# Shifting SBUF buffers by pads of 32 to 224 bytes in an attention + two-layer FFN kernel on one core

## The chip, the core and the metric

The kernel runs on one core of a Trainium2 chip. The metric is device time in microseconds (us), the median of three runs. SBUF is addressed here in bytes within a partition (all 128 partitions of a buffer have the same address), and "residue" always means that address modulo 256.

## What is computed

The reference, cut to its core, for 8 batches x 8 heads x 576 tokens, a head size of 64 and so a model width of 512, with an inner width of 1536 in both layers:

```python
kv  = einsum('bhsd,bhse->bhde', k, v)            # linear attention, no softmax
a   = einsum('bhsd,bhde->bhse', q, kv)
a   = a / sqrt(mean(a*a, -1) + 1e-6) * g_norm    # 4608 tokens x 512 after the heads are joined
x   = (sigmoid(a @ w_gate) * (a @ w_val)) @ w_out
g   = x @ w2_gate
out = (g * sigmoid(g) * (x @ w2_val)) @ w2_out
```

## The kernel before

**Arithmetic.** Every matrix product of the two layers is done with each float32 operand split into a rounded "hi" part and a "lo" remainder, and three products (lo*hi, hi*lo, hi*hi). The tokens go in 9 blocks of 512 (`j`). The inner width of one layer is cut into 12 tiles of 128; `PH` makes four stages of them: stage 0 is the first 6 tiles of layer 1 in plain form, stage 1 the other 6 tiles of layer 1, stages 2 and 3 the two halves of layer 2. In stages 1 to 3 two tiles make a pair, and the gate and value products of a pair go through a Winograd-like scheme with seven products (`gv_win`); in stage 3 the out product does too (`out_win`).

**The matmul lines.** A matmul reads two SBUF operands: the stationary one is loaded into the array by a weight load of its own (128 columns of 4 bytes, 512 bytes a partition), and the moving one streams through. The lines are: L645 (`gv_plain`, stage 0; stationary gate/val weights `wgv`, moving `x`, 512 columns), L716 (`gv_win`, stages 1 to 3; stationary `wgv`, moving `x`, 256 columns, 84 matmuls for one pair of one block, called a visit here), L813 (`part_plain`, the out product of stage 0; stationary `wo`, moving `h`, 512 columns), L827 (`part_win`, the out product of stages 1 and 2, 24 matmuls a visit, 512 columns; in stage 1 `wo` is stationary and `h` moves, in stage 2 `h` is stationary and `wo` moves), and L848 (`out_win`, stage 3, 256 columns; `h` stationary, `wo` moving). While one matmul streams, the weight load of the next one reads SBUF beside it.

**Order.** PE's order is written out by hand: each visit's gate/val matmuls come first, then the out matmuls of the visit before (`tail`). From block 4 of stage 0 on, the orders of ScalarE, VectorE and GpSimd are by hand as well. SP's queue issues nearly all DMAs, paced by `tick`.

**Where the buffers lie.** Pools stack up from the left end of SBUF (`hp_` with `h`, then `wk`, `sm`, then `w0p` and `x0p`, which `late_l` replaces after stage 0) and down from the right end (`at`, which `late_r` replaces once the attention is done). A tile begins where the one before it ends; `h` begins at byte 1152, behind constants and DMA scratch, and `late_r` ends at byte 229344. In stage 0, weights, `x` and `wo` lie in `w0p` and `x0p`. In stages 1 to 3 there are six weight slots `s`: slots 0 and 1 lie in `late_r` (called wR below), slots 2 to 5 in `late_l` (wL). A visit of the first pair uses wR, a visit of the other two pairs wL. The 14 parts of `x` lie in `late_r` (xR: tiles x0, x1, x2) for one block and in the `arena` tile of `late_l` (xA) for the next; stage 1 begins with xR, stage 2 with xA, and stage 3 uses xR throughout. So the 81 visits are 18 of xR with wR, 36 of xR with wL, 9 of xA with wR and 18 of xA with wL. The out weights `wo` of slots 0 and 1 are tiles of `late_r`, those of slots 2 to 5 lie in the arena. In stage 3 all out weights lie in the arena; the 42 parts of `h` that a block's three visits make lie in `h` itself (18 parts of one block, 324 matmuls over the stage), in two `raw` slots of `wk` or in the two free `wo` slots of `late_r` by turns (`he`, 336 and 312 matmuls), and in the `xl` slots of `wk` (`hl`, 162 matmuls).

All sizes are multiples of 32 bytes, and within a tile both operands advance by whole multiples of 512 bytes, so the residue of a tile's start is that of each operand taken from it.

Of the kernel before, what the change touches and what calls it, by code (L numbers as in the profile page):

```python
# [9 lines left out]
F32 = mybir.dt.float32  # L10
F32R = mybir.dt.float32r
# [9 lines left out]
def attention_two_ffn(ctx: ExitStack, tc: tile.TileContext, q, k, v, g_norm, weights, out):  # L21
# [10 lines left out]
    DM = H * D  # L32
    DFF = weights[0][0].shape[1] // 2
    NT = B * S
    P = 128
# [3 lines left out]
    KD = DM // P  # L39
    NP = H // 2  # L40
    R = 4
    KB = 1024
# [4 lines left out]
    hp_ = ctx.enter_context(tc.tile_pool(name="hp", bufs=1))  # L47
# [3 lines left out]
    ps_o = ctx.enter_context(tc.tile_pool(name="ps_o", bufs=4, space=PSUM))  # L51
    ps_g = ctx.enter_context(tc.tile_pool(name="ps_g", bufs=4, space=PSUM))

    lo_ctx, at_ctx = ExitStack(), ExitStack()
    w0p = lo_ctx.enter_context(tc.tile_pool(name="w0p", bufs=1))
    x0p = lo_ctx.enter_context(tc.tile_pool(name="x0p", bufs=4))
    at = at_ctx.enter_context(tc.tile_pool(name="at", bufs=1, side="right"))
    late = {}
# [5 lines left out]
    def open_left():  # L64
        lo_ctx.close()
        late["L"] = ctx.enter_context(tc.tile_pool(name="late_l", bufs=1, reuse_waits="tile"))
        for m in range(PH[1][1] + 2, PH[1][1] + 6):
            w_tile(0, m, 0)
        late["arena"] = late["L"].tile([P, 11 * KB], F32R, name="arena")


    ET = mybir.EngineType
# [23 lines left out]
    for j in range(NBLK):  # L96
        t = dr.tile([DM, NB], F32, name=f"xd{j}")
# [148 lines left out]
    def tok_c(tau):  # L246
        if tau >= XT:
            t = xn.pop(tau).rearrange("p h d -> p (h d)")
            z = at.tile([P, DM // SQ, SQ], F32, tag="ta", bufs=TA, name="xz")
            nc.vector.transpose(z.rearrange("p j c -> p (j c)"), t)  # L250
            j, c = divmod(tau, TPB)
            for i in range(P // SQ):
                t0 = c * P + i * SQ
                nc.sync.dma_start(out=xr[j][:, :, t0:t0 + SQ], in_=z[i * SQ:(i + 1) * SQ])
            return
        t = xn.pop(tau).rearrange("p (a b) d -> p a (b d)", b=2)
        ps = bank_for(tau < TPB, "xTp")
        for hp in range(NP):
            nc.tensor.transpose(ps[:, hp, :], t[:, hp, :], ident)  # L259
        x = at.tile([P, NP, P], F32, tag="ta", bufs=TA, name="xT")  # L260
        nc.scalar.activation(x, ps, AF.Identity, scale=gcol)
        j, c = divmod(tau, TPB)
        cs = slice(c * P, (c + 1) * P)
        if j < 2:
            xh, xlo = x_tiles(0, j)
            nc.scalar.activation(xh[:, :, cs], x, AF.Copy)  # L266
            (nc.gpsimd if j == 0 and c < TPB - 1 else nc.vector).tensor_tensor(out=xlo[:, :, cs], in0=x, in1=xh[:, :, cs].bitcast(F32), op=ALU.subtract)
        nc.scalar.dma_start(out=xd[0, j][:, :, cs], in_=x)
# [55 lines left out]
    NRIGHT = 2  # L324
# [16 lines left out]

    wgv, wo, wd = {}, {}, {}

    def w_tile(f, m, c):
        d = wo if c == 2 else wgv
        if (f, m) not in d:
            ph, s = phase_of[f, m]
            pool = w0p if ph == 0 else late["R" if s < NRIGHT else "L"]
            if c == 2 and ph in WOUT:
                a = 3584 * (s // 2)  # L350
                d[f, m] = d[f, m ^ 1] = late["arena"][:, a:a + 3584].rearrange("p (q a) -> p q a", a=2 * P)
            elif c == 2 and ph and s >= NRIGHT:
                a = 7 * KB + (s - NRIGHT) * KB
                d[f, m] = late["arena"][:, a:a + KB].rearrange("p (b a) -> p b a", b=2)
            elif c == 2:
                d[f, m] = pool.tile([P, 2, DM], F32R, tag=f"wo{s}", name=f"wo{f}_{m}")
            elif PH[ph][3]:
                d[f, m] = pool.tile([P, 14, 2, P], F32R, tag=f"wgv{s}", name=f"wgv{f}_{m}")
            else:
                d[f, m] = pool.tile([P, 2, 2, KD, P], F32R, tag=f"wgv{s}", name=f"wgv{f}_{m}")  # L360
        return d[f, m]

    def rounded(f, m, c, buf):
# [36 lines left out]
    def direct(f, m, c):  # L400

        third = (3 * m + c) % 3 == 0

        def buf(t):
            pool = at if third and t != "s" else wk
            if t == "raw":
                return pool.tile([P, DM, 2], U32, tag=t, name=t)
            return pool.tile([P, DM], F32, tag=t, name=t)

        load, ops_, st = rounded(f, m, c, buf)  # L410

        def dst(b):
            t = w_tile(f, m, c)
            return (t[:, b], st["u"]) if c == 2 else (t[:, c, b], st["u"].rearrange("p (k a) -> p k a", k=KD))

        def hi():
            h, u = dst(0)
            nc.scalar.activation(h, u, AF.Copy)

        def lo():  # L420
            h, u = dst(0)
            (nc.vector if m == 0 and c < 2 else nc.gpsimd).tensor_tensor(out=dst(1)[0], in0=u, in1=h.bitcast(F32), op=ALU.subtract)

        return load, ops_ + [hi, lo]
# [113 lines left out]
    def place(f, m):  # L538

        E = 14 * 2 * P  # L540

        def load_gv():
            t = w_tile(f, m, 0).rearrange("p q k a -> p (q k a)").bitcast(F32)
            nc.sync.dma_start(out=t, in_=wd[f, m][:, :E])

        def load_o():
            t = w_tile(f, m, 2).rearrange("p b a -> p (b a)").bitcast(F32)
            nc.sync.dma_start(out=t, in_=wd[f, m][:, E:])

        return load_gv, load_o  # L550
# [3 lines left out]
    xt, xc = {}, {}  # L554
    HB = NB // 2

    def x_load(ph, j, b):
        for i in (b, b + 7):
            t = x_tiles(ph, j)[i // 5][:, i % 5].rearrange("p k a -> p (k a)").bitcast(F32)
            nc.sync.dma_start(out=t, in_=xc[j][:, i * DM:(i + 1) * DM])  # L560

    def x_tiles(ph, j):
        if (ph, j) not in xt:
            if PH[ph][3]:
                s = "RL"[((ph - 1) * NBLK + j) % 2]
                if ph in WOUT and j:
                    xt[ph, j] = x_tiles(ph, 0)
                elif s == "L":
                    xt[ph, j] = [late["arena"][:, i * 5 * DM:min(i * 5 + 5, 14) * DM].rearrange("p (c k a) -> p c k a", k=2, a=HB) for i in range(3)]
                else:  # L570
                    xt[ph, j] = [late[s].tile([P, 5 - i // 2, 2, HB], F32R, tag=f"x{i}", name=f"x{i}") for i in range(3)]
            else:
                xt[ph, j] = [x0p.tile([P, KD, NB], F32R, tag="x", name=f"x{b}") for b in range(2)]
        return xt[ph, j]
# [55 lines left out]
    ht, ops, part, pd = {}, {}, {}, {}  # L630


    h_all = hp_.tile([P, 2, 2, 3, HB], F32R, name="h")
    h_at = [0]

    def gv_plain(ph, j, m, tick):
# [23 lines left out]
    def h_places():  # L660
        if not hw:
            raw = [wk.tile([P, 4, HB], F32R, tag="raw", name="he") for _ in range(2)]
            own = [late["R"].tile([P, 4, HB], F32R, tag=f"wo{i}", name="he") for i in range(2)]
            hw["E"] = raw, own
            flat = h_all.rearrange("p a b c d -> p (a b c) d")
            far = [wk.tile([P, 2, HB], F32R, tag="xl", bufs=3, name="hl") for _ in range(3)]
            hw["L"] = [[flat[:, 6 * p + 2 * i:6 * p + 2 * i + 2] for i in range(3)] for p in range(2)] + [far]
            hw["n"] = 0
        return hw

    def gv_win(ph, j, m, tick, ahead=nop):
# [76 lines left out]
        gated(v[:, 0], v[:, 0], g)  # L748
        if ph in WOUT:
            pl = h_places()  # L750
            p = (m - PH[ph][1]) // 2
            E, Lt = pl["E"][pl["n"] % 2], pl["L"][p]
# [407 lines left out]
    for ph, (f, m0, n, win) in enumerate(PH):  # L1160
# [4 lines left out]
        for at_, (j, ms) in enumerate(visits):  # L1165
# [6 lines left out]
            for i in ms:  # L1172
# [6 lines left out]
                m = m0 + i  # L1179
# [15 lines left out]
                if win:  # L1195
                    ahead = nop
                    if tail and tail[0] in WOUT and tail[2] + 2 == PH[tail[0]][1] + PH[tail[0]][2]:
                        parts = parts_of(tail)
                        ahead = parts.pop(0)
# [22 lines left out]
        if not win:  # L1222
            held = []
            early.__exit__(None, None, None)
            early = tc.manual_schedule(engines={ET.PE, ET.Activation, ET.DVE, ET.Pool, ET.SP})
            early.__enter__()
            finish(parts_of(tail), 0, 0)
            tail = None
            open_left()
            for s in range(NRIGHT, PH[ph + 1][2], 2):  # L1230
                put_place(ph + 1, s, 0, 1 + s // 2)
                if s == NRIGHT:
                    for e in range(2):
                        w_need((f, PH[ph + 1][1] + s + e, 0))
                    for store in held:
                        store()
                    held = None
                put_place(ph + 1, s, 2, 2 + s // 2)
# [31 lines left out]
```

## Time and profile before

| | us |
|---|---|
| median of 3 runs (1805.06 to 1805.45) | 1805.35 |
| span of the profiled execution (first to last instruction) | 1803.8 |
| PE matmul busy, of that span | 1781.5 (99%) |
| PE weight loads busy | 1630.9 (90%) |
| VectorE, ScalarE, GpSimd busy | 1059.3, 659.9, 682.9 |
| L716 visits, stages 1 to 3 (6804 matmuls) | 549.3 + 274.2 |
| L645, stage 0 gate/val (1296 matmuls) | 316.3 |
| L813, L827, L848 out products (648, 1296, 1134 matmuls) | 164.5; 310.8; 148.6 |

A busy PE does not say at what rate matmuls follow each other: matmuls overlap in the pipeline, and the mean duration of one in the table of groups (282 ns for 256 columns) is longer than the distance from one to the next. That distance is read from the chain of waits, which merges an unbroken run of matmuls into one piece and gives its time and count: 9.94 us for 84 matmuls is 118.3 ns for each.

### The profile page before, as it was taken

To read this page: it belongs to the slowest core of one execution; us is meant where nothing else is said; L and a number is where in the kernel's file an instruction comes from. 1 tells how busy PE (TensorE), PEld (TensorE's weight loads), DVE (VectorE), ACT (ScalarE), POOL (GpSimd) and SP (SyncE) were. 2 spreads that over 40 slices of the span, in tenths; PEclk is the share of its full clock that TensorE was granted. 3 is DMA by queue.
4 is the path that set the end of the run, shared out by engine and by line. 5 is a ranking of instruction groups with operands and counts; after the bars stand their busy time and mean duration, and the time that the engine had idled before them with its cause. 6 is when DMAs were issued, how large, how long until landed. Compare 5 with 4: busy or idle time off the path is not lost.

```text
span 1803.8 us, 31990 instructions
## 1 busy us (share of the span) xinstructions
PE 1781.5 (99%) x12358; PEld 1630.9 (90%) x12358; DVE 1059.3 (59%) x1754; ACT 659.9 (37%) x1349; POOL 682.9 (38%) x748
## 2 busy tenths in 40 slices
PE   7899999999999999999999999999999999999999
PEld 6788888888889999999999999999999999999998
DVE  6766566654336667666666566655553555555555
ACT  4663233333233333333333443333432333333332
POOL 1644445421013343342433443333441344444444
PEclk9999999999999999999999999999999999999999
DMA  9968785456326542433449755555568634344432
GB/s 291 264 171 230 222 221 161 133 146 229 105 94 257 181 135 94 157 110 115 145 139 402 271 191 178 181 180 185 186 233 304 216 129 129 129 129 129 129 129 71
DMA packets 274825, 320.40 MB, mean 178 GB/s; under 512 B 95856, under 2 KB 193392, under 8 KB 271984
## 3 DMA queue, kind: packets, MB, share of 16 engines
q1 hardware_dynamic: 259504, 305.24, 52.3%
q10 hardware_dynamic: 15168, 13.11, 2.5%
q8 instruction: 97, 1.59, 0.4%
q14 instruction: 56, 0.46, 0.1%
HBM read 191.14 MB, written 127.14 MB: 176 GB/s over the span
## 4 chain that ended last, share of the span: by engine, by line
PE 95%; DMA 2%; DVE 1%; ACT 1%; SPq 0%; POOL 0%; issue 0%; DVEq 0%; ACTq 0%
PE gv L716 45%; PE o L827 17%; PE gv L645 16%; PE o L813 8%; PE o L848 7%; PE ops L212 1%; DMA raw<-in_moe_w_gate_dram 1%; PE kvps L162 1%; DMA raw<-in_moe_w_out_dram 1%; DMA qm<-in_q_dram 0%; PE xTp L259 0%; DMA pl<-pd 0%; SPq L109 0%; DMA xd<-xT 0%; PE qTp L196 0%
## 5 line engine op out<-in xcount | busy, mean ns | idle before, releaser
L716 PE MATMUL gv<-x,wgv 128*128 128x256 f32 x4536 | 549.3, 282 | 0.0
L716 PEld LDWEIGHTS gv<-x,wgv 128*128 128x128 f32 x4536 | 545.5, 189 | 2.8 <-DVE v L332 0.2
L645 PE MATMUL gv<-x,wgv 128*128 128x512 f32 x1296 | 316.3, 395 | 3.7 <-ACT x L266 2.7
L645 PEld LDWEIGHTS gv<-x,wgv 128*128 128x128 f32 x1296 | 241.3, 189 | 55.6 <-ACT x L266 3.2
L716 PEld LDWEIGHTS gv<-arena,wgv 128*128 128x128 f32 x2268 | 273.6, 190 | 2.4
L716 PE MATMUL gv<-arena,wgv 128*128 128x256 f32 x2268 | 274.2, 282 | 0.0
L332 DVE TENSOR_TENSOR u<-u,gv 128x512 f32<-128x512 f32 x162 | 110.9, 684 | 259.9 <-PE gv L716 247.7
L704 POOL TENSOR_TENSOR h<-v,h 128x512 fp32r<-128x512 f32 x54 | 75.0, 1389 | 241.5 <-ACT h L700 241.2
L813 PE MATMUL o<-h,wo 128*128 128x512 f32 x648 | 164.5, 397 | 0.0
L689 ACT ACTIVATE w<-v 128x256 f32<-128x256 f32 x81 | 33.9, 418 | 312.3 <-DVE v L332 305.0
L813 PEld LDWEIGHTS o<-h,wo 128*128 128x128 f32 x648 | 120.0, 188 | 26.7 <-issue 0.3
L704 POOL TENSOR_TENSOR h<-w,h 128x512 fp32r<-128x512 f32 x54 | 70.8, 1311 | 139.5 <-ACT h L700 138.9
L653 DVE TENSOR_TENSOR sg<-sg,gv 128x512 f32<-128x512 f32 x54 | 36.9, 684 | 114.3 <-PE gv L645 114.3
L827 PE MATMUL o<-arena,h 128*128 128x512 f32 x432 | 103.6, 395 | 0.0
L827 PE MATMUL o<-h,arena 128*128 128x512 f32 x432 | 103.3, 394 | 0.0
L827 PEld LDWEIGHTS o<-arena,h 128*128 128x128 f32 x432 | 79.9, 188 | 17.9
L827 PEld LDWEIGHTS o<-h,arena 128*128 128x128 f32 x432 | 80.1, 188 | 17.5
L760 POOL TENSOR_TENSOR he<-w,he 128x256 fp32r<-128x256 f32 x27 | 20.0, 740 | 186.5 <-ACT he L759 186.5
L848 PE MATMUL o<-arena,he 128*128 128x256 f32 x648 | 82.1, 281 | 0.0
L689 ACT ACTIVATE v<-g 128x256 f32<-128x256 f32 x81 | 33.8, 418 | 131.5 <-DVE g L332 131.5
L332 DVE TENSOR_TENSOR g<-u,gv 128x512 f32<-128x512 f32 x81 | 55.6, 687 | 43.5 <-PE gv L716 42.0
L700 ACT ACTIVATE h<-w 128x512 fp32r<-128x512 f32 x54 | 34.1, 631 | 124.9 <-PE o L827 87.0
(145 smaller groups left out, 2643.2 us busy)
## 6 DMA issues: line engine op xcount, KB each, us to landing
wgv<-wd SPq DMA_DIRECT2D x18, 1792.0 KB, 9.9
x<-xc SPq DMA_DIRECT2D x126, 256.0 KB, 4.2
pl<-pd SPq DMA_DIRECT2D x80, 256.0 KB, 4.0
pd<-ye SPq DMA_DIRECT2D x72, 256.0 KB, 2.7
xc<-arena SPq DMA_DIRECT2D x70, 256.0 KB, 3.3
wd<-raw SPq DMA_DIRECT2D x63, 256.0 KB, 2.9
xc<-x SPq DMA_DIRECT2D x56, 256.0 KB, 3.6
raw<-in_moe_w_gate_dram SPq DMA_DIRECT2D x24, 512.0 KB, 4.5
```

The source lines that it names most:

```text
L162: nc.tensor.matmul(kvps[b][e * D:(e + 1) * D, hp, :D], lt, rt, start=(r == hp == 0), stop=(r == R and hp == NP - 1), skip_group_check=True)
L332: nc.vector.tensor_tensor(out=out, in0=a, in1=b, op=ALU.add)
L645: nc.tensor.matmul(ps, w[:, e, a, kk, :], x[b][:, kk, :], start=(n == 0), stop=(n == 3 * KD - 1))
L653: nc.vector.tensor_tensor(out=sg, in0=sg, in1=bank[1], op=ALU.mult)
L689: nc.scalar.activation(o, t[:, 0], AF.Silu if f else AF.Sigmoid)
L700: nc.scalar.activation(t[:, 0], v, AF.Copy)
L704: nc.gpsimd.tensor_tensor(out=t[:, 1], in0=v, in1=t[:, 0].bitcast(F32), op=ALU.subtract)
L716: nc.tensor.matmul(ps[:, e], w[:, l, kk], xs[r // 5][:, r % 5, kk], start=(fresh and e == n == kk == 0), stop=(not more and e == 1 and n = ...
L760: nc.gpsimd.tensor_tensor(out=hs[z][:, 1], in0=x, in1=hs[z][:, 0].bitcast(F32), op=ALU.subtract)
L813: nc.tensor.matmul(ps, l, r, start=(fresh and t == 0), stop=(last and t == 2))
L827: nc.tensor.matmul(ps, l, r, start=(fresh and e == t == 0), stop=(last and e == 1 and t == 2))
L848: nc.tensor.matmul(ps[:, t], h[:, r, cs], w[:, Ax[a] + 7 * l], start=(start and t == n_ == 0), stop=(stop and t == 1 and n_ == 2), skip_gr ...
```

## The change

A helper `shifted` allocates a tile with some elements ahead of it and behind it that nobody uses, and returns the part between. `LINE` is 8 elements, 32 bytes. `h` moves up by 128 bytes and a 224-byte tile follows it, so everything left of the middle moves up by 352 bytes; the first weight tile of stage 0 gets 160 bytes ahead, weight slot 2 gets 128 ahead, the arena 32 ahead, weight slot 1 gets 32 behind, and x2 of `late_r` 224 behind. No instruction, wait or DMA is added or taken away in the kernel's own code.

The residues that follow, each worked out by adding up the tile sizes:

| buffer | before | after |
|---|---|---|
| stage 0: wgv, wo, x | 0, 0, 0 | 0, 0, 0 |
| h | 128 | 0 |
| tiles of wk (raw, xl, u, v, w, s ...) | 128 | 224 |
| wL | 0 | 224 |
| wR | 224 | 224 |
| xA and the out weights in the arena | 0 | 0 |
| xR | 224 | 0 |
| wo slots of late_r (and he in them) | 224 | 0 |

The stationary operand's residue less the moving one's is written as a difference below. The gate/val visits before: xR with wR 0, xR with wL +32, xA with wR -32, xA with wL 0; after: -32 in all four. The out products before: L813 128; L827 128 with arena weights, 96 or -96 with `wo` of `late_r`; after: 0 in all of them. L848 before: 128, and -32 for the 312 matmuls with `he` in `late_r`; after: 0 with `h` itself and with `he` in `late_r`, -32 with `raw` and `hl`.

```diff
+    def shifted(pool, cols, dtype, by, name, tag=None):
+        ahead, after = by if isinstance(by, tuple) else (by, 0)
+        t = pool.tile([P, ahead + cols + after], dtype, name=name, **({"tag": tag} if tag else {}))
+        return t[:, ahead:ahead + cols]
+
+    LINE = 8
+    H_AT, ARENA_AT, X_AFTER = 4 * LINE, LINE, 7 * LINE
+    RIGHT, LEFT = {(1, 0): (0, LINE)}, {2: 4 * LINE}
+    FIRST = {(0, 0): 5 * LINE}
...
-        late["arena"] = late["L"].tile([P, 11 * KB], F32R, name="arena")
+        late["arena"] = shifted(late["L"], 11 * KB, F32R, ARENA_AT, "arena")
...
+    def w_shift(ph, s, c):
+        if ph:
+            return RIGHT.get((s, c // 2), 0) if s < NRIGHT else LEFT.get(s, 0)
+        return FIRST.get((s, c // 2), 0)
...
-                d[f, m] = pool.tile([P, 14, 2, P], F32R, tag=f"wgv{s}", name=f"wgv{f}_{m}")
+                d[f, m] = shifted(pool, 28 * P, F32R, w_shift(ph, s, c), f"wgv{f}_{m}", f"wgv{s}").rearrange("p (q k a) -> p q k a", k=2, a=P)
...
-                    xt[ph, j] = [late[s].tile([P, 5 - i // 2, 2, HB], F32R, tag=f"x{i}", name=f"x{i}") for i in range(3)]
+                    xt[ph, j] = [shifted(late[s], (10 - i // 2 * 2) * HB, F32R, (0, X_AFTER * (i // 2)), f"x{i}", f"x{i}").rearrange("p (c k a) -> p c k a", k=2, a=HB) for i in range(3)]
...
-    h_all = hp_.tile([P, 2, 2, 3, HB], F32R, name="h")
+    h_all = shifted(hp_, 12 * HB, F32R, H_AT, "h").rearrange("p (b e s a) -> p b e s a", b=2, e=2, s=3)
+    hp_.tile([P, 7 * LINE], F32, name="gap")
```

The tiles `wo`, the stage 0 `wgv` and the `he` tiles in the `wo` slots go through `shifted` in the same way.

## Rows read from the trace of the kernel before

**Rows 1.** The page: busy time of the engines, TensorE's granted clock, the chain.
```profile
PE 1781.5 (99%) x12358; PEld 1630.9 (90%) x12358; DVE 1059.3 (59%) x1754; ACT 659.9 (37%) x1349; POOL 682.9 (38%) x748
PEclk9999999999999999999999999999999999999999
PE 95%; DMA 2%; DVE 1%; ACT 1%; SPq 0%; POOL 0%; issue 0%; DVEq 0%; ACTq 0%
```

**Rows 2.** Busy time by stretch: stretch, its length, engines (instructions), clock, DMA.
```profile
138.00:230.00 92.00, 91.21 (x593) 75.72 (x592) 51.84 (x85) 32.27 (x58) 39.20 (x64) 1.00 0.85 225
230.00:548.00 318.00, 318.00 (x1511) 261.93 (x1510) 165.35 (x256) 104.13 (x188) 94.89 (x125) 1.00 0.53 154
554.00:1450.00 896.00, 895.98 (x6290) 837.46 (x6289) 548.85 (x888) 333.08 (x674) 342.46 (x288) 1.00 0.54 191
```

**Rows 3.** The chain from 579 us, stage 1: start, duration, matmuls in a piece.
```profile
579.59 9.94 PE gv L716 x84
589.53 5.57 PE o L827 x24
595.11 9.80 PE gv L716 x84
604.90 5.57 PE o L827 x24
610.48 10.07 PE gv L716 x84
620.55 5.61 PE o L827 x24
626.16 10.06 PE gv L716 x84
...
641.80 10.07 PE gv L716 x84
```

**Rows 4.** The chain from 1134 us, stage 2.
```profile
1150.63 5.60 PE o L827 x24
1156.22 9.90 PE gv L716 x84
1166.12 5.60 PE o L827 x24
1171.72 10.07 PE gv L716 x84
1181.79 5.62 PE o L827 x24
```

**Rows 5.** The chain from 490 us, the end of stage 0.
```profile
490.65 2.79 PE o L813 x12
493.44 5.45 PE gv L645 x24
498.89 2.79 PE o L813 x12
501.69 5.46 PE gv L645 x24
```

**Rows 6.** The chain in stage 3, from 1473 us and from 1518 us.
```profile
1473.42 2.85 PE o L848 x24
1476.27 8.63 PE gv L716 x72
...
1518.29 2.81 PE o L848 x24
```

**Rows 7.** Busy time inside four visits of stage 1, columns as in group 2.
```profile
645.00:651.00 6.00, 6.00 (x53) 6.00 (x52) 3.22 (x6) 0.80 (x2) 1.92 (x3) 1.00 0.00 1
598.00:604.00 6.00, 6.00 (x54) 6.00 (x53) 3.37 (x6) 0.80 (x2) 0.60 (x1) 1.00 0.69 226
629.00:635.00 6.00, 6.00 (x53) 6.00 (x52) 5.38 (x10) 1.00 (x3) 0.53 (x1) 1.00 0.00 0
```

**Rows 8.** PE in order of time around 200 us, and L813's matmuls before 201 us.
```profile
201.63 3.04 PE L645 MATMUL gv<-x,wgv 128*128 128x512 f32 x12 [0.79 <-DVE xn L242]
...
92.00:201.00 109.00, 33.23 (x126) 22.48 (x124) 1.00 0.76 205
```

**Rows 9.** SP's queue and PE in order of time around 550 us, and DMA landings there.
```profile
545.61 0.90 SPq L544 DMA_DIRECT2D wgv<-wd  x2
...
553.80 20.17 PE L716 MATMUL gv<-x,wgv 128*128 128x256 f32 x168
...
wgv<-wd SPq DMA_DIRECT2D x4, 1792.0 KB, 12.2
```

**Rows 10.** DMA landings from 400 to 425 us, the first loads of wR.
```profile
wgv<-wd SPq DMA_DIRECT2D x2, 1792.0 KB, 9.2
```

More of the change, by code (lines that the diff above doesn't have):

```diff
@@ L355, in w_tile @@
             elif c == 2:
-                d[f, m] = pool.tile([P, 2, DM], F32R, tag=f"wo{s}", name=f"wo{f}_{m}")
+                d[f, m] = shifted(pool, 2 * DM, F32R, w_shift(ph, s, c), f"wo{f}_{m}", f"wo{s}").rearrange("p (b a) -> p b a", b=2)
             elif PH[ph][3]:
-                d[f, m] = pool.tile([P, 14, 2, P], F32R, tag=f"wgv{s}", name=f"wgv{f}_{m}")
+                d[f, m] = shifted(pool, 28 * P, F32R, w_shift(ph, s, c), f"wgv{f}_{m}", f"wgv{s}").rearrange("p (q k a) -> p q k a", k=2, a=P)
             else:
-                d[f, m] = pool.tile([P, 2, 2, KD, P], F32R, tag=f"wgv{s}", name=f"wgv{f}_{m}")
+                d[f, m] = shifted(pool, 4 * KD * P, F32R, w_shift(ph, s, c), f"wgv{f}_{m}", f"wgv{s}").rearrange("p (c b k a) -> p c b k a", c=2, b=2, k=KD)
         return d[f, m]
@@ L662, in h_places @@
             raw = [wk.tile([P, 4, HB], F32R, tag="raw", name="he") for _ in range(2)]
-            own = [late["R"].tile([P, 4, HB], F32R, tag=f"wo{i}", name="he") for i in range(2)]
+            own = [shifted(late["R"], 4 * HB, F32R, w_shift(1, i, 2), "he", f"wo{i}").rearrange("p (c a) -> p c a", a=HB) for i in range(2)]
             hw["E"] = raw, own
```

## The prediction

> **What bounds the kernel now.** I read the page first: PE is busy 99% of the span, at the full granted clock in every slice, and 95% of the chain that ends last is PE [rows 1]. Next comes the busy time by stretch, which tells where that is so: from 230 us to 548 and from 554 to 1450, PE has no idle time worth a number, while the next engine, VectorE, is busy about half or three fifths of it [rows 2]. So from 201.6 us on, behind the last wait of stage 0 that shows [rows 8], a nanosecond less between one matmul and the next is a nanosecond off the end, as long as nobody makes PE wait.
>
> The third view is the chain of waits, because it gives unbroken runs of matmuls with their count. Divide a piece's time by its count and the distance between matmuls comes out. The reader is to see that visits of identical work, 84 matmuls of L716 with 256 columns, take three or four different times, and that these go with the buffers read. Stage 1 runs, in order, xR/wL 9.94, xA/wR 9.80, xA/wL 10.07, xA/wL 10.06, xR/wR 10.07 us [rows 3]. Per matmul that is 118.3, 116.7, 119.9 and 119.9 ns. By difference of residues: +32 gives 118.3, -32 gives 116.7, 0 gives 119.9. In stage 2 the two equal ones stay at 10.07 and -32 gives 9.90 (117.9) [rows 4]; in stage 3, 72 matmuls of xR/wR take 8.63, again 119.9 each [rows 6].
>
> Three things speak for the residues as the cause. xR/wR and xA/wL share no buffer, lie some 100 KB apart, and agree to 0.1%. Inside the visits the other engines and the DMA differ widely without a trace in the rate: in the xA/wL visit VectorE works 5.38 of 6 us, in the xR/wR one 3.22, both at 119.9, and the fast visit has the most DMA of the three, a share of 0.69 [rows 7]. And the clock is 1.00 in all of them.
>
> The 512-column lines show the same thing with another sign. L645 (0/0, difference 0) takes 5.45 to 5.46 us for 24, 227.2 ns; L813 right beside it (difference 128) takes 2.79 for 12, 232.5 ns [rows 5]. L827 takes 5.57 to 5.62 for 24, 232.1 to 234.2 [rows 3, 4]. So for 512 columns an equal residue is the best pair that shows, and for 256 columns it is the worst.
>
> The Trainium skill speaks against this: its page "SBUF — State Buffer", section "SBUF: two separate sides", says that only the port pair shared by VectorE and GpSimd causes contention and that PE never waits on anyone, and "TensorE: Matmul & The Clock Gate", section "Step-by-step: what each phase is for", says that loading the next weights takes no SBUF read bandwidth from the running matmul. By that rule a pad costs and gives nothing and the time stays at 1805.4; the 10.07 against 9.80 of equal visits [rows 3] disagrees.
>
> **The change part by part.** It adds no instruction, no DMA and no wait of its own; it only moves residues. Terms are worked out against the profiled span of 1803.8 us; the median lies 1.55 us above it, and I carry that over.
>
> Gate/val visits (L716). All 81 come to -32. Today's -32 visits take 9.80 in stage 1 (5 of them) and 9.90 in stage 2 (4), mean 9.85; I take the mean and keep both ends. The 18 xR/wR visits fall from 10.07 to 9.85, 4.0 us; the 18 xA/wL ones the same, 4.0; the 36 xR/wL ones from 9.94 to 9.85, 3.2; the 9 xA/wR ones stay. Together 11.2 us. If all settle at 9.80, 81 x 0.05 = 4.1 us more; if all at 9.90, 4.1 less.
>
> Out products of stages 1 and 2 (L827), difference 0 in all 1296. Their six rows here average 5.59 us, 233.1 ns [rows 3, 4]; the nearest row for 512 columns at difference 0 is L645, 227.2. That is 5.9 ns x 1296 = 7.6 us. No row shows L827 itself at 0, so the bounds are 0 (it stays as it is) and 8.5 us (from its slowest rows, 234 against 227.2, a little rounded).
>
> Out products of stage 0 (L813), difference 0. 5.3 ns x 648 = 3.4 us, but 126 matmuls plus some fifteen before them lie ahead of the wait at 201.6 us, where PE waits 0.79 us for VectorE [rows 8]: being faster before it only makes that wait longer. 507 x 5.3 = 2.7 us is left, with bounds 0 and 3.4.
>
> Out products of stage 3 (L848). At 128 today 24 matmuls with `he` in `raw` take 2.85 us, at -32 with `he` in `late_r` 2.81 [rows 6]. The two swap roles in part: 336 + 162 matmuls go from 128 to -32, 0.04/24 us each, 0.8 us gained; 312 go from -32 to 0 and 324 from 128 to 0. No row shows L848 at 0; the nearest is L716's 119.9 ns, against 117.1 and 118.75 now, so 0.9 and 0.4 us are lost. Net 0.5 us lost; bounds 1.3 lost and 0.8 gained (if 0 costs nothing).
>
> Pads as such. A late tile now covers other bytes, and so may wait for another old tile (the arena's first bytes reach into stage 0's weight tile 4). That tile is read before tile 5, on which the arena waits anyway, so this costs nothing. The cover is the slack of the first wL loads: issued by 546.5 us, landing in 12.2 us (median) [rows 9], so at 558.7, and read when the first xR/wR visit ends, some 10.1 us after 553.8 us, at 563.9. About 5 us are free, and PE gets there only 0.2 us earlier. If the new destination residue made these loads slow, up to that slack is hidden; wR, already at 224, landed in 9.2 us [rows 10], so nothing points to it.
>
> Other engines read and write the moved `wk`, but with VectorE at three fifths and PE 1.2% faster, nothing on them comes near the end.
>
> Sum: 11.2 + 7.6 + 2.7 - 0.5 = 21.0 us. 1803.8 - 21.0 = 1782.8 us of span, and a time of 1784.3 us.
>
> **The rivals.**
> (a) The period is longer than 256. All three classes of today hold modulo 512 too, since their differences there are 0, +32 and -32. Modulo 512 the new starts are xR 256, wR 224, xA 0, wL 480, `h` 256, `wo` of `late_r` 256. Then xR/wR and xA/wL still come to -32 (8.0 us), xR/wL and xA/wR land at an unseen 224 (taken as today's middle, 9.94: 0 and 9 x 0.09 = 0.8 us lost), and of the out products only the 432 with `wo` of `late_r` become equal (2.5 us); the rest stay, with 0.5 lost in stage 3. That is 9.2 us, 1796.2. For it: no row tells 256 from 512. Against it: nothing in the rows either; only that the pairs agree at any distance.
> (b) Only the gate/val part works, because L645's 227 ns belong to its own pattern of operands and not to the residue: 11.2 - 0.5, 1794.7. Against it: L645 reads the same shapes with the same alternation of hi and lo parts.
> (c) No effect, because the rates come from something that goes along with the buffers (or by the skill's rule): 1805.4. Against it, all of rows 3 to 6.
> (d) Slower: every gate/val weight slot shares residue 224 with the `wk` tiles that VectorE, ScalarE and GpSimd stream through during the visits, and weight loads pay for it. No row shows this pair; today's xR/wR visits share 224 only with each other. It decides when a visit exceeds its present mean of 9.99 by the 9.8 us that the rest gives, so at 10.11 (120.4 ns). If it cost one more step of the kind seen (10.07 - 9.80) on top of the slowest class, 10.34, the visits lose 81 x 0.35 = 28 us and the time is 1824. Against it: the rate does not follow VectorE's work [rows 7].
>
> **How the numbers follow.** The forecast has a chance of 0.78, (a) 0.08, (b) 0.06, (c) 0.05, (d) 0.03. Its own range, from the ends above, is 21.0 + 4.1 + 0.9 + 0.7 + 1.3, so 1777.3, to 21.0 - 4.1 - 2.7 - 0.8, so 1792.0; the end where L827 gains nothing is (b). To hold 8 in 10, I take 1778.5 to 1796.5, which reaches (a) and (b). A measurement of this kernel can tell about 0.2% (3.6 us) from no change. The forecast, (a) and (b) are all faster: 0.91 with a little of each below the bound taken off; same 0.06; slower 0.03.
>
> **What would show it.** In the profile after: all L716 visits between 9.80 and 9.90 us; L827 at 5.45 for 24 and L813 at 2.73 for 12; L645 unchanged at 5.45; L848's pieces mixed, 2.81 to 2.88 for 24; no new idle time of PE at 563.9 us. Visits of xR/wL and xA/wR that differ from xR/wR and xA/wL would show (a); L827 still at 5.59 would show (b). What would make me wrong outright is a matmul rate that depends on more than the residue and the width, or a PE wait that shows only once PE is faster.

## The result, and the profile after

The changed kernel takes 1782.01 us (median of 4 runs, 1781.64 to 1782.27) where the kernel before took 1805.29 beside it (4 runs): a ratio of 0.9869 [0.9857, 0.9881], 23.3 us less. The forecast was 1784.3. The profiled execution has a span of 1779.9 us against 1803.8. All lines below L645 have moved: L660 is the old L645, L731 the old L716, L828 the old L813, L842 the old L827, L863 the old L848, and L338 and L341 are VectorE's helpers.

The page of the changed kernel, busy time of the engines, answers [rows 1]:

```profile
PE 1757.9 (99%) x12358; PEld 1616.1 (91%) x12358; DVE 1060.0 (60%) x1754; ACT 660.7 (37%) x1349; POOL 683.2 (38%) x748
```

The same instructions, PE just as full, the other engines as busy as before: only the matmuls follow each other faster. The chain of waits shows where (start, duration, matmuls in a piece): stage 1, which answers [rows 3], then stage 2 [rows 4], the end of stage 0 [rows 5] and stage 3 [rows 6].

```profile
549.90 19.60 PE gv L731 x168
...
574.97 9.80 PE gv L731 x84
584.77 5.47 PE o L842 x24
590.24 9.80 PE gv L731 x84
600.05 5.47 PE o L842 x24
605.52 9.80 PE gv L731 x84
...
1126.70 9.80 PE gv L731 x84
1136.50 5.47 PE o L842 x24
...
471.01 2.72 PE o L828 x12
473.73 5.44 PE gv L660 x24
...
1440.43 2.87 PE o L863 x24
1443.30 9.80 PE gv L731 x84
1453.10 2.80 PE o L863 x24
1455.90 8.40 PE gv L731 x72
```

Visits that took 9.80, 9.90, 9.94 or 10.07 us before all take 9.80 now, 116.7 ns a matmul, with any pair of buffers and in all three stages. L842 takes 5.47 for 24, 227.9 ns, where L827 took 5.57 to 5.62. Stage 1 begins 3.9 us earlier (549.90 against 553.80 [rows 9]); the other 20 us come behind it. The first piece is unbroken over both of its visits, so the first loads of wL hold nobody up.

If every matmul is counted from its start to the start of the next one and these distances are summed by line over the whole trace, the difference of spans, 23.9 us, comes apart like this:

| line (before / after) | before, us | after, us | gained | forecast |
|---|---|---|---|---|
| L716 / L731, the visits | 809.25 | 795.65 | 13.6 | 11.2 |
| L827 / L842, out of stages 1, 2 | 302.05 | 295.62 | 6.4 | 7.6 |
| L813 / L828, out of stage 0 | 156.25 | 153.25 | 3.0 | 2.7 |
| L645 / L660, gate/val of stage 0 | 303.9 | 302.8 | 1.1 | 0 |
| L848 / L863, out of stage 3 | 134.0 | 134.1 | -0.1 | -0.5 |
| sum | | | 24.0 | 21.0 |

One new entry stands in the view of waits (total us, times, longest), for PE's weight loads:

```profile
PEld gv L731 <- DVE v L341: 1.5, 5, 0.5
```

Five visits of stage 1 now wait for VectorE, 1.5 us in all (0.2 us in one visit before). The 13.6 us are what is left behind this: 81 visits at 9.80 come to 793.8, which would have been 15.1 us below the 808.9 that the pieces of before add up to.

### The profile page after: what moved, and what is told of

Same layout as the page of the kernel before. It is cut to its first block, busy times and chain, and to the rows that moved or that the text cites. A ratio compares the mean times of both kernels' runs of the same rounds, so it can differ in the third digit from the quotient of the medians.

```text
span 1779.9 us, 31991 instructions
## 1 busy us (share of the span) xinstructions
PE 1757.9 (99%) x12358; PEld 1616.1 (91%) x12358; DVE 1060.0 (60%) x1754; ACT 660.7 (37%) x1349; POOL 683.2 (38%) x748
## 4 chain that ended last, share of the span: by engine, by line
PE 92%; DVE 3%; DMA 2%; issue 1%; ACT 1%; SPq 1%; POOL 1%; DVEq 0%; ACTq 0%
PE gv L731 43%; PE o L842 16%; PE gv L660 15%; PE o L828 8%; PE o L863 7%; PE ops L221 1%; PE kvps L171 1%; DMA raw<-in_moe_w_out_dram 0%; DMA qm<-in_q_dram 0%; PE xTp L268 0%; DVE u L341 0%; DVE pl L341 0%; SPq L118 0%; DMA pl<-pd 0%; DVE u L400 0%
## 5 line engine op out<-in xcount | busy, mean ns | idle before, releaser
L731 PE MATMUL gv<-x,wgv 128*128 128x256 f32 x4536 | 539.7, 279 | 0.4 <-DVE v L341 0.3
L731 PEld LDWEIGHTS gv<-x,wgv 128*128 128x128 f32 x4536 | 535.9, 188 | 3.2 <-DVE v L341 0.8
L660 PE MATMUL gv<-x,wgv 128*128 128x512 f32 x1296 | 313.8, 393 | 3.5 <-ACT x L275 2.4
L660 PEld LDWEIGHTS gv<-x,wgv 128*128 128x128 f32 x1296 | 240.3, 188 | 53.5 <-ACT x L275 2.9
L731 PEld LDWEIGHTS gv<-arena,wgv 128*128 128x128 f32 x2268 | 268.8, 188 | 3.0 <-DVE v L341 0.7
L731 PE MATMUL gv<-arena,wgv 128*128 128x256 f32 x2268 | 269.8, 279 | 0.1
L341 DVE TENSOR_TENSOR u<-u,gv 128x512 f32<-128x512 f32 x162 | 110.9, 684 | 244.8 <-PE gv L731 232.8
L828 PE MATMUL o<-h,wo 128*128 128x512 f32 x648 | 161.9, 394 | 0.3 <-DVE h L338 0.3
L828 PEld LDWEIGHTS o<-h,wo 128*128 128x128 f32 x648 | 120.0, 188 | 25.1 <-DVE h L338 0.7
L842 PE MATMUL o<-h,arena 128*128 128x512 f32 x432 | 101.4, 390 | 0.0
L842 PE MATMUL o<-arena,h 128*128 128x512 f32 x432 | 101.4, 390 | 0.0
L842 PEld LDWEIGHTS o<-h,arena 128*128 128x128 f32 x432 | 79.8, 188 | 15.9
L842 PEld LDWEIGHTS o<-arena,h 128*128 128x128 f32 x432 | 79.8, 188 | 15.9
L863 PE MATMUL o<-arena,he 128*128 128x256 f32 x648 | 82.2, 281 | 0.0
L341 DVE TENSOR_TENSOR g<-u,gv 128x512 f32<-128x512 f32 x81 | 55.6, 687 | 41.4 <-PE gv L731 40.1
L863 PEld LDWEIGHTS o<-arena,he 128*128 128x128 f32 x648 | 79.0, 189 | 0.0
```

The costliest lines, as they stand in the source:

```text
L341: nc.vector.tensor_tensor(out=out, in0=a, in1=b, op=ALU.add)
L660: nc.tensor.matmul(ps, w[:, e, a, kk, :], x[b][:, kk, :], start=(n == 0), stop=(n == 3 * KD - 1))
L731: nc.tensor.matmul(ps[:, e], w[:, l, kk], xs[r // 5][:, r % 5, kk], start=(fresh and e == n == kk == 0), stop=(not more and e == 1 and n = ...
L828: nc.tensor.matmul(ps, l, r, start=(fresh and t == 0), stop=(last and t == 2))
L842: nc.tensor.matmul(ps, l, r, start=(fresh and e == t == 0), stop=(last and e == 1 and t == 2))
L863: nc.tensor.matmul(ps[:, t], h[:, r, cs], w[:, Ax[a] + 7 * l], start=(start and t == n_ == 0), stop=(stop and t == 1 and n_ == 2), skip_gr ...
```

## The experiments

Each edit is shown against the changed kernel; numbers in the code are elements of 4 bytes. In these kernels `GAP` is the length of the tile behind `h`, `X_AHEAD` what x0 gets ahead of it, and keys (0, 0), (0, 1) of `RIGHT` are the weights and the `wo` of slot 0. `SLOT` is what the two `wo` slots of `late_r` get ahead. Values of `LEFT`, `FIRST` and `RIGHT` are left out where they only put another buffer back to its residue, or, in the three sweeps, give each weight slot a residue of its own. Differences are residue of the stationary operand less that of the moving one, as before. Where a rate of a whole line or visit is given to a tenth of a ns, it is a mean of distances between starts.

**Half of the change at a time.** First the gate/val part alone: all visits at -32, while `h`, `wk` and the late `wo` keep the residues of before.

```diff
-    H_AT, ARENA_AT, X_AFTER = 4 * LINE, LINE, 7 * LINE
+    H_AT, GAP, ARENA_AT = 0, 0, 8
+    X_AHEAD, X_AFTER = 8, 56
...
-    hp_.tile([P, 7 * LINE], F32, name="gap")
```

> The gate/val half of the change alone: all weight slots 32 bytes below both x buffers (difference -32), while h, wk and the out weights keep the residues of before (differences 128 and +-96 in the out products). Residue theory: L716 takes 9.80 us a visit, 13.6 us less over 81 visits than before, and L827 stays at 5.57 to 5.62 for 24: 1791.7 us. Sub-question, what sets 9.80 against 9.90 at the same difference: if it is the out product that runs just before the visit, stage 2's visits of wR with the arena's x go back to 9.90 as before, and the time is up to 2.7 us longer, 1794.4; if it is something else, all 81 stay at 9.80. Rival (b) of the prediction gives the whole gain to this half: 1782. Rival that the pads act through something other than the residues: no definite place for the gain, anything from 1782 to 1805.

1791.79 us (1791.13 to 1793.0; before 1806.01), ratio 0.9922 [0.9906, 0.9939]. The chain in stage 1, and two pieces of stage 2:

```profile
578.78 9.80 PE gv L732 x84
588.58 5.58 PE o L843 x24
...
619.34 5.63 PE o L843 x24
624.96 9.90 PE gv L732 x84
...
1149.87 9.80 PE gv L732 x84
1159.67 5.57 PE o L843 x24
```

The visits fall and the out products stay where they were. 9.90 appears again, but not where it did before: all 27 visits of stage 2 take 9.80, and 9.90 stands in 5 visits of stage 1, each behind an L843 at +96 (four more visits behind +96 take 9.80), and in 8 of stage 3. So -32 has two rates, and the stage does not choose between them.

Then the out part alone: gate/val buffers as before, all out products as after.

```diff
+    H_AT, GAP, ARENA_AT = 32, 56, 0
+    X_AHEAD, X_AFTER = 56, 0
```

> The out half alone: h, wk and the out weights as in the changed kernel (difference 0 in L813 and L827), while the gate/val residues are those of before (x and wR at 224, wL and the arena at 0). Residue theory: visits of 10.07, 9.94, 9.80 to 9.90 and 10.07 us as before, L827 at 5.47 for 24 (6.4 us less in all), L813 at 2.72 for 12 (3.0 less), L645 about 1 us less: 1794.8 us, and the gains of both halves add up to the whole, 23.3. Rival (b): 1805.

1796.31 us (1795.81 to 1798.71; before 1806.01), ratio 0.9949 [0.9934, 0.9964]. The chain in stage 1:

```profile
575.29 9.94 PE gv L733 x84
585.23 5.47 PE o L844 x24
590.71 9.80 PE gv L733 x84
600.51 5.46 PE o L844 x24
605.97 10.07 PE gv L733 x84
```

The mirror image: 9.94, 9.80 and 10.07 as before, 5.47 as after. The parts gain 14.2 and 9.7 us, 23.9 together, the whole gain within its error. One thing crosses over: here the nine visits at -32 all take 9.80, those of stage 2 too, where four of them took 9.90 [rows 4]. Of what PE reads, only the operands of the out products between them differ.

**The wk tiles.** `wk` put back to 128, all else as after; this is rival (d), weights that share residue 224 with what the other engines stream through.

```diff
+    H_AT, GAP, ARENA_AT = 32, 32, 8
```

> The changed kernel with the wk tiles at 128 as before in place of 224; all differences of gate/val and of L813 and L827 as in the changed kernel, but he in raw and hl at +128 in L848 as before. Rival (d) of the prediction (weights that share a residue with wk pay for it) would make the visits faster than 9.80; the residue theory leaves them at 9.80 and makes L848 slower by 498 x 1.7 ns = 0.8 us: 1783.

1784.25 us (1783.3 and 1785.19; before 1805.56), ratio 0.9882 [0.9863, 0.9902]. Visits stay at 9.80 (eight of stage 3 at 9.90), and L848's matmuls with `raw` and `hl`, now at 128, go from 116.9 to 118.9 ns. Sharing a residue with `wk` costs nothing; `wk` matters only as an operand of stage 3.

**Other differences.** Three kernels put every buffer at a place of its own, so that one kernel shows many differences: steps of 32 bytes, steps of 16 bytes, and a mixture.

```diff
+    H_AT, GAP, ARENA_AT = 56, 32, 32
+    X_AHEAD, X_AFTER = 48, 32
```

> A sweep of differences in steps of 32 bytes. Gate/val: arena x at 0 with weights at 192, 160, 128 (differences -64, -96, 128), the other x at 96 with the same weights (+96, +64, +32). h at 96: L827 at -96 and +96 with arena weights, +64 and -64 with the others; stage 0's six weight slots at 0 to 160 against x at 0 (L645) and against h at 96 (L813, -96 to +64). Residue theory: +32 comes out at 9.94 a visit as in the kernel before although other buffers and residues make it, 128 at 118.7 ns (9.97), the rest unseen, inside 9.80 to 10.07; L813 at 0 (slot 3) 2.72 for 12, at the others 2.76 to 2.81. Time 1790 to 1806. Rival that absolute residues or the buffers set the rate: no order by difference, +32 anywhere between 9.80 and 10.07.

```diff
+    H_AT, GAP, ARENA_AT = 36, 52, 60
+    X_AHEAD, X_AFTER = 32, 8
```

> The same in steps of 16 bytes. Gate/val: arena x at 0 with weights at 240, 208, 16 (differences -16, -48, +16), the other x at 192 (+48, +16, +80). h at 16: L827 at -16, +16 with arena weights, +48 and -48 with the others; L645 at -16, +16, +48, +80, +112, +144; L813 at -32, 0, +32, +64, +96, +128. Residue theory: +16 takes the same time with both x buffers (two places, two pairs of residues, one difference); if -32 is the bottom of a smooth hollow, -16 and -48 lie between 9.80 and 9.95; if the rate steps in units of 32 bytes, -16 equals 0 or -32. Time 1788 to 1806.

```diff
+    H_AT, GAP, ARENA_AT = 32, 56, 36
+    X_AHEAD, X_AFTER = 8, 48
```

> Differences that are still missing, with h, wk and the order of SP as in the changed kernel: arena x and the arena's out weights at 16, gate/val weights at 0, 96 and 128 (differences -16, +80, +112), the other x at 32 (-32, +64, +96). Residue theory: -32 at 116.7 and +64 at 113.9 to 114.5 in a third and fourth place, +96 at 118.25 as in the first sweep, the new ones unseen; L827 with arena weights at -16 and +16, between 228 and 234. Time 1782 to 1800, since no PE wait comes with it.

1875.33, 1878.92 and 1786.25 us, one run each. The first two missed by 70 us and more, for a reason that has nothing to do with the rates (below, `h` alone). In the second, the differences were not those designed, since the built kernel has every tile's length rounded up to 32 bytes; it adds little. Visits in stage 2 of the first kernel, in order -64, -96, +96 and +64:

```profile
1045.57 9.89 PE gv L733 x84
...
1061.08 10.08 PE gv L733 x84
...
1092.24 9.97 PE gv L733 x84
...
1107.83 9.54 PE gv L733 x84
```

and of the third kernel, a visit at -16 in stage 1, then -16, -32 and +64 in stage 2:

```profile
589.58 9.97 PE gv L733 x84
...
1146.00 9.53 PE gv L733 x84
...
1192.10 10.08 PE gv L733 x84
1207.74 9.54 PE gv L733 x84
```

With other buffers at other residues, +32 gives 118.3 ns again, so the difference counts and not the buffers. But it does not give one rate. Over all kernels here but the second sweep, one matmul of a visit takes:

| difference | rates seen, ns |
|---|---|
| 0 | 120.0 |
| +32 | 118.3 |
| -32 | 116.7, 117.8, 120.0 |
| +64 | 113.3, 117.8 (117.3 where a visit changes its rate, see below) |
| -64 | 117.8 |
| +96; -96 | 117.3, 118.6, 120.0; 120.0 |
| 128 | 118.6 (in the second sweep also 120.0) |
| -16; +80; +112 | 113.3, 118.6; 119.3; 118.7 |

Most visits keep one of these almost from start to end. For 512 columns 0 is the best seen, 227 to 228 ns (up to 230.2 where other differences stand beside it); -64 takes 229.5 to 232, -16 and +16 231.6, the others 232 to 234.

**The fastest rate, +64.** 113.3 ns would save 81 x 0.27, 22 us. So all gate/val buffers went to +64, the rest as after.

```diff
+    H_AT, GAP, ARENA_AT = 32, 56, 48
+    RIGHT = {(0, 0): 24, (0, 1): 48}
```

> The changed kernel with the gate/val weights 64 bytes above x (difference +64) in place of 32 below, all else as in the changed kernel. In the 32-byte sweep the pair at +64 took 114.5 ns for a matmul, in the 16-byte one another pair of buffers at +64 took 113.85. Residue theory: visits of 9.56 to 9.62 us against 9.80, 81 x 0.2 = 16 us less than the changed kernel, 1766 us, if VectorE keeps up; the changed kernel already has five waits of stage 1 for VectorE, 1.3 us in all, and these should grow: up to 8 us if each of the 12 visits to the arena's x in stage 1 lost half of its gain and more, 1774. Rival that 114 ns came from the slower surroundings of those two runs (PE waiting elsewhere, other engines less busy): visits stay at 9.80, 1782.

1782.08 us (1781.62 to 1783.89; before 1805.24), ratio 0.9876 [0.9859, 0.9892]: no better than the change, and the expectation fell. The chain in stage 1, and a visit in stage 3:

```profile
575.11 9.89 PE gv L733 x84
585.01 5.46 PE o L844 x24
590.47 9.89 PE gv L733 x84
...
1478.48 9.53 PE gv L733 x84
```

All 54 visits of stages 1 and 2 took the slow rate, 117.8 (four of them up to a pause, see below); in stage 3 the 17 behind an L848 at -32 took 113.3 and the 8 behind one at 0 took 117.8. That suggested that the out product in between picks the rate. Two kernels tried it: stage 3's out products at +64 too, and the out products of stages 1 and 2 at +96 and -96, behind which the first sweep had shown 113.3.

```diff
+    H_AT, GAP, ARENA_AT = 32, 16, 48
...
+            own = [shifted(late["R"], 4 * HB, F32R, (SLOT[i] + 16, 48), "he", f"wo{i}").rearrange("p (c a) -> p c a", a=HB) for i in range(2)]
...
+            flat = h_t[:, H_AT + 16:H_AT + 16 + 12 * HB].rearrange("p (n d) -> p n d", d=HB)
```

> As the one with +64, and stage 3's out product too: h, the wk slots and the he places stand 64 bytes above the out weights in stage 3 alone (a second view of h, 64 bytes further on), all 1134 matmuls of L848 at +64. Residue theory: L848 falls from 118.4 ns (mean of the changed kernel) to about 114, 1134 x 4.3 = 4.9 us less than with the gate/val part alone, some 1761. Rival that +64 is good for gate/val streams only: no difference from it.

```diff
+    H_AT, GAP, ARENA_AT = 32, 32, 48
+    RIGHT = {(0, 0): 0, (0, 1): 48}
+    SLOT = (48, 0)
+    X_AHEAD, X_AFTER = 0, 16
```

> Gate/val weights 64 bytes above x as in the kernel with +64, but the out products of stages 1 and 2 at -96 and +96 (x and all late out weights at 160, the gate/val weights at 224, h at 0), and in stage 3 the he and hl places 32 below the out weights. In the runs so far +64 has two rates, 113.3 and 117.8 ns, and keeps the one it begins with: 113.3 in 13 of 13 visits behind an L827 at +-96 and in 25 of 29 behind an L848 at -32 or -48, 117.8 in almost all behind a difference of 0. Theory that the out product just before picks the rate: visits of 9.52 us all through, 81 x 0.28 = 23 us less than the changed kernel, L827 at 5.60 in place of 5.47, 54 x 0.13 = 7 us more, L848 some 1 us less, waits for VectorE in stage 1 up to 5 us more: 1765 to 1771 us. Rival that the absolute residues pick it: 117.8 as in the kernel with +64, 1789.

1787.86 us (1786.67 to 1789.02), ratio 0.9905 [0.989, 0.992], and 1784.75 (1783.86 to 1785.5; before 1805.56), ratio 0.9884 [0.9867, 0.99]. Both expectations fell, and so did their rivals. With everything at +64, gate/val and out products of stage 3 run at 117.8 throughout. With out products at +96 and -96, the visits of stages 1 and 2 still take 9.89, though the same differences gave 9.54 in the sweep; behind L848 at -32 again 25 of 25 take 113.3. From stage 1 of the second kernel, and from its stage 3:

```profile
575.32 9.89 PE gv L734 x84
585.21 5.61 PE o L845 x24
...
1485.09 9.52 PE gv L734 x84
1494.61 2.80 PE o L866 x24
```

So what ran before a visit matters, but the difference of the out product alone does not settle it. Nor do the residues of the visit's own operands: in the second kernel the same two (`x` at 160, weights at 224) take 117.8 in stages 1 and 2 and 113.3 in stage 3. The traces show one thing more: a pause can change the rate inside a visit. In the kernel with +64 this line of the weight loads stands in a visit of stage 1:

```profile
706.51 1.45 PEld L733 LDWEIGHTS gv<-arena,wgv 128*128 128x128 f32 x12 [0.24 <-DVE v L343]
```

The 70 matmuls ahead of the pause follow each other at 117.8 ns; from the sixth behind it on they follow at 113.3, with the same buffers and the same difference. In four kernels visits at +64 have such a pause near their end, 15 in all, and in 14 of them this is so. So the rate also goes with how the matmuls and weight loads stand in time when a stretch begins; what sets that stays open.

**h alone.** `h` moved by 64 or by 32 bytes, with everything else where the change puts it.

```diff
+    H_AT, GAP, ARENA_AT = 48, 40, 8
```

> The changed kernel with h alone moved, to residue 64 (differences +-64 in L813 and L827, +64 in L848 with h). SP's order of DMAs is that of the changed kernel. Residue theory: L827 at 232 to 234 ns and L813 the same in place of 228, 1944 x 5 = 10 us more, L848 with h at 114 in place of 119.4 gives 1.7 back: 1790. Rival for the slowness of the two sweeps, that an h at another residue than 0 or 128 makes the engines that write or read it slow: some 50 us of PE waits as there, 1840.

```diff
+    H_AT, GAP, ARENA_AT = 40, 48, 8
```

> The changed kernel with h at residue 32. This alone changes the order in which the build puts SP's DMAs in stage 1 (23 places from the 389th on; no order changes with h at 0, 64 or 128), as in the two sweeps. Theory that this order made the sweeps slow: PE waits of 50 to 60 us for h in stage 1 as there, 1840 to 1860 us, with the rates of L716 still 116.7 ns. Rival that the sweeps were slow for their many pads or their mix of differences: about 1792, the 10 us of the out products at +-32 alone.

1789.35 us and 1872.51, one run each. The first is the time that was expected, but not by its terms: the out products of stages 0 to 2 lost 5.5 us in place of 10, L645 beside them 2.2 where nothing was expected, and L848 gave back 0.9 for 1.7. The two kernels differ in eight elements ahead of `h` and eight behind it. In the slower one PE waits for `h` (total us, times, longest):

```profile
PE o L844 <- ACT h L717: 36.2, 13, 4.7
PE o L844 <- POOL h L721: 11.8, 13, 2.1
```

The engines in order of time show what it waits for. First the slower kernel, then the same visit with `h` at 64:

```profile
594.34 0.61 ACT L717 ACTIVATE h<-v 128x512 fp32r<-128x512 f32 x1
595.00 0.80 PE L844 MATMUL o<-h,arena 128*128 128x512 f32 x1 [3.62 <-ACT h L717]
596.44 1.44 POOL L721 TENSOR_TENSOR h<-v,h 128x512 fp32r<-128x512 f32 x1
597.93 8.23 PE L844 MATMUL o<-h,arena 128*128 128x512 f32 x23 [2.14 <-POOL h L721]
...
588.15 5.67 PE L844 MATMUL o<-h,arena 128*128 128x512 f32 x24
591.35 0.61 ACT L717 ACTIVATE h<-v 128x512 fp32r<-128x512 f32 x1
593.51 1.49 POOL L721 TENSOR_TENSOR h<-v,h 128x512 fp32r<-128x512 f32 x1
```

With `h` at 64, L844 begins 3.2 us before ScalarE writes this part of `h` and ends before GpSimd has written it, so it does not read it: the part belongs to the visit in progress, while L844 works on the visit before. With `h` at 32, L844 waits for both writes all the same. The part lies right behind the two that L844 reads, and they share no byte. The programs differ in this: the built one with `h` at 32 has such waits in 13 places, and so have the two slow sweeps, while the nine other kernels here and the kernels before and after have none. What the three have in common is that `h` begins 32 or 16 bytes off a multiple of 64 bytes; why the build then adds the waits is not shown. The order of DMAs on SP's queue also differs in these three, in 23 of 1059 places. The theory on record, that this order makes them slow, forecast 1840 to 1860 us, but the waits above account for the idle time without it.

The waits come to 48 us; against `h` at 64 the kernel loses 83. Part of the rest is the clock. The busy time by stretch, columns as in group 2 of before, behind the second wait above:

```profile
598.00:601.00 3.00, 3.00 (x7) 2.41 (x8) 0.00 (x0) 0.00 (x0) 1.11 (x1) 0.50 1.02 383
```

PE stood still for 3.62 and 2.14 us before, and the granted clock here is the lower of its two levels, 1.2 GHz in place of 2.4: seven matmuls in 3 us, 427 ns each in place of 233. Behind eleven of the 13 pairs of waits the 23 matmuls take 7.0 to 8.2 us in place of 5.4, which makes some 23 us over all of them. The remaining 12 us are not taken apart here.

**What the runs point to.** -32 held 116.7 behind an out product at 0, and +64 held 113.3 in stage 3 behind one at -32. So: stages 0 to 2 as in the change; in stage 3 `x` 160 bytes higher in its tiles, which makes the visits +64, and `h` and `he` 32 bytes lower than their places, which makes all of L848 -32.

```diff
+                    x_up = 5 * LINE if ph in WOUT else 0
...
+            own = [shifted(late["R"], 4 * HB, F32R, (SLOT[i] + 7 * LINE, LINE), "he", f"wo{i}").rearrange("p (c a) -> p c a", a=HB) for i in range(2)]
...
+            flat = h_t[:, H_AT - LINE:H_AT - LINE + 12 * HB].rearrange("p (n d) -> p n d", d=HB)
```

> The changed kernel as it is in stages 0 to 2 (-32 and 0). In stage 3 alone x stands 160 bytes higher in its tiles (gate/val difference +64), and h and he in late_r move so that all 1134 matmuls of L848 are at -32. In two kernels before, +64 took 113.3 ns in stage 3 behind an L848 at -32 (17 of 17 and 25 of 25 visits). Theory that the stream before picks the rate: 27 visits at 9.55 us in place of 9.80 (7 us), L848 at 116.8 ns in place of 119.5 for 636 matmuls (1.7 us): 1773.3 us. Rival that the rate one gets at +64 can't be foreseen from the stream before: 117.8 ns in stage 3, 2.6 us lost and 1.7 won, 1783.

1773.92 us (1772.31 to 1774.94, 5 runs; before 1805.05), ratio 0.9826 [0.9813, 0.984], which beats both kernels. The page and the chain in stage 3:

```profile
PE 1746.7 (99%) x12358; PEld 1605.1 (91%) x12358; DVE 1060.8 (60%) x1754; ACT 660.1 (37%) x1349; POOL 681.9 (38%) x748
```

```profile
1473.29 9.54 PE gv L736 x84
1482.83 2.80 PE o L868 x24
1485.63 9.54 PE gv L736 x84
```

All 27 visits of stage 3 take 113.3 ns, and all of L848 116.7 to 116.9. 27 x 0.27 is 7.3 us, and 636 matmuls x 2.6 ns another 1.7: 9.0 against the 8.1 us between this kernel and the changed one. Here a rate was chosen from the table and its neighbour with it, and it came. That the neighbour brought it is not shown: two of the 27 visits stand behind an out product of stage 2 at 0, behind which +64 had taken 117.8 throughout in the kernel with +64, and they take 113.3 too.

## Why the prediction came out as it did

**What bounds the kernel** held: PE stayed at 99%, and of what the faster rates gave only the 1.5 us of new waits for VectorE did not come off the span.

**The residues as the cause** held. The two halves of the change gave two separable gains in the lines whose residues they moved, and `+32` gave its rate again with other buffers. By the Trainium skill, page "TensorE: Matmul & The Clock Gate", section "Step-by-step: what each phase is for", loading the next weights takes no read bandwidth from the running matmul; here residues alone, at one granted clock and with the same instructions, change the distance between matmuls by 2.7% (119.9 to 116.7 ns for the pairs that had difference 0), so rival (c) is out. That the two reads of PE meet somewhere in SBUF is still only argued: no run separates the weight load from the moving read.

**L716** was mis-sized, 11.2 for 13.6 us. I took the mean of the two rates that -32 had in the trace of before, 9.85, for a property of the stages; all 81 visits took the faster. The trace of before spoke against this already: the five visits at 9.80 were the four of stage 1 and one of the five in stage 2, and not five of stage 1. It goes with what runs around a visit instead: at -32 behind an out product at 0, every visit of the changed kernel, and of the kernel with the out part alone, takes 9.80, while out products left as before brought 9.90 back in 13 of 81. So the two parts, which I costed apart, touch each other there. 1.5 us of it went into waits for VectorE, which I had named only as a thing that could go wrong, without a price.

**L827** was priced at 227.2 ns, the rate of L645, and came to 228.1, 6.4 us for 7.6: the row was the right one, off by 0.9 ns. Rival (b), that this rate belongs to L645's pattern, is out.

**L813** gained 3.0 us for 2.7. **L645** gained 1.1 where I had none, since its own residues do not move; its rate went from 228.2 to 227.4 ns. With the gate/val part alone it stays at 228.1 and with the out part alone it is 227.4, so it goes with the L813 beside it: the same neighbour effect, which I left out.

**L848** lost 0.1 for 0.5. 498 matmuls went from 118.7 to 116.9 (0.9 us gained), 312 from 117.2 to 119.5 and 324 from 118.7 to 119.5 (0.7 and 0.3 lost). L716's 119.9 was a good stand-in for difference 0.

**Rival (a)** is refuted by the changed kernel itself: all four pairs take 9.80. **Rival (d)** has neither its price in the changed kernel nor a gain when `wk` is put back. **The pads as such** cost nothing here: no wait at 563.9 us. That was true of these lengths; with `h` 32 bytes further on, the built program had waits in 13 more places and the time was 1872.51, 67 us more than before the change. My costing of the pads looked at the bytes they cover and not at this.

That the time came so close is in part luck, since errors of both signs met. In sum the forecast of 21.0 us was 3.0 too small: 2.4 too little on L716, 1.1 on L645, 0.4 on L848 and 0.3 on L813, 1.2 too much on L827. The time came out only 2.3 us under the forecast, because the median lies 2.1 us above the profiled span now, where I had carried over 1.55.

## What to carry to other kernels

Where PE is full, divide the pieces of the chain by their matmuls; if identical work runs at several rates, list for each the addresses of both operands modulo 256 before looking for another cause. Read a new placement's rate from a run with the same neighbours, not from a mean over rows with others, and price the lines next to the moved ones too. A pad may also change the waits that a build puts into the program, so look in the view of waits for an engine that waits for something it does not read, and keep to lengths that add no wait.

## What was unexpected of the hardware

One difference can have two or three rates (113.3 and 117.8 ns at +64; 116.7, 117.8 and 120.0 at -32), most often kept through a visit of 84 matmuls; what ran before bears on which, and a pause of some 0.2 to 0.5 us inside a visit at +64 turned 117.8 into 113.3. The best difference for 256 columns is not the best for 512: 0 always takes the slowest rate seen for the one (120.0) and is the fastest for the other (227 to 228). And short waits of PE, 3.62 and 2.14 us, were followed by matmuls of 427 ns instead of 233 at the lower granted clock (0.50), so that waits of 48 us went with a loss of 83.
